# Separate query and key buffers, each reloaded on its own, in a fused attention and gated feed-forward kernel

## The chip, the cores and the metric

The kernel runs on one core of one Trainium2 chip. The metric is the device time of one launch in microseconds (us). Three runs before the change gave 353.80, 353.83 and 354.33 us, median 353.83. The profiled execution spans 352.2 us from its first to its last instruction, with a mean granted TensorE clock of 0.997.

Names used below: TensorE is PE in the profile, its weight loads PEld, VectorE DVE, ScalarE ACT, GpSimd POOL, SyncE SP. A "q" after an engine's name (SPq) is its sequencer, which issues transfers and waits for semaphores.

## The reference, cut to what matters

```python
# q, k, v: (8, 12, 448, 64) f32 ; x: (3584, 768)
q_n, k_n = rmsnorm(q, g_q), rmsnorm(k, g_k)           # over the last 64
attn = softmax(q_n @ k_n.T / 8)                       # 96 heads, 448 x 448
x = (attn @ v).transpose(0, 2, 1, 3).reshape(3584, 768)
a, b = x @ w1, x @ w2                                 # (768, 1024) each
out = (a * b) @ w3 @ w_out                            # (1024, 1024), (1024, 768)
```

Nothing lies between the two last products, so the kernel multiplies the weights w3 and w_out once (w34) and applies the result.

## The kernel before, in words

**Tiles.** The work is cut into 24 "quads" of four heads (three quads make one of the 8 batch entries). A quad's queries and keys are loaded as two transfers of 448 KB into one array `qk_sb`, of which there are three, used in turn (`qk_bufs[i % 3]`, line 308; the second axis of the array tells query from key). So quad i+3 reloads the array of quad i.

**Preparation of a quad** (`plan_prep`, line 455). ACT squares queries, then keys (L464, tile `sq`); DVE sums them (L471, `ssq`); ACT makes the factor by a logarithm and an exponential (L480, L483, `al`); DVE scales queries and keys, in two pieces each (L494, `qks`), and multiplies the queries by the gains (L503). The first five quads (`N_PE_T`) are transposed on TensorE (L1123) and copied out of PSUM into `qkT` (L358 on DVE or L352 on ACT); the others by a DMA transpose that SP issues (L561).

**Attention of a quad.** Seven score passes on TensorE (L679, four matmuls of 64x64 weights and 448 columns each) into two PSUM banks, each followed by an exponential on ACT (L701, into `P` or `Pr`). Then the products with the values and the sums of the rows (L745 and L766), the reciprocals on ACT (L788, L789) and the multiplication into `xT` on DVE (L808), which frees the banks. These products are mostly made for two quads together.

**Feed-forward.** When three quads of a batch entry are in `xT`, its products with w1 and w2 become available, and later those with w34. All of them, and w3 by w_out at the start, run through `do_pass` (L868): four matmuls of 64x64 weights, into a pair of banks. A pair of sums changes its row halves midway, and the change goes through a no-operation on SP or POOL (L852), called a hand-over below. Results leave PSUM by L352 or L358 into `half`, or by L949 (the product a times b, `abT`). Stores are issued by SP (L1005).

**What sets the order.** No engine's order is written out by hand. While the program is built, a planner (`Planner`, line 46) keeps a list of jobs, each with an assumed duration, a rank and conditions; it always takes the job that can start first, and so fixes each engine's order. TensorE takes what `pe_try` (line 1241) offers: scores, a feed-forward pass, a transpose, value products. On the chip each engine runs its list strictly in that order, waiting on semaphores. Where an assumed time is missed on the chip, TensorE stands at the head of its list although later work could run. A few constants steer `pe_try`: `STARVED` (few waiting pairs, below which scores are taken more eagerly) and `HOLD` (if set, value products of two quads wait while a pair of sums is open and no other pair could start).

**Loads.** The weights, the values and the queries and keys of quads 1 to 5 go through POOL, in the order of `POOL_ORDER` (o is a part of w_out, w of w3, a of w1, b of w2, q and v with the quad's number). From quad 6 on SP loads queries and keys. The load of quad i+3 is planned in `complete` (L565), when queries and keys of quad i are both scaled, and may start at `qk_free[i % 3]`, which is set when the last of the four scaling pieces is done. Values are held in four buffers (`v_sb`, L407).

Of the kernel before, what the change touches and what calls it, by code (L numbers as in the profile page):

```python
# [8 lines left out]
FP = mybir.dt.float32  # L9
# [3 lines left out]
AF = mybir.ActivationFunctionType  # L13
# [7 lines left out]
SEM = 0.05  # L21
# [174 lines left out]
def kernel(  # L196
# [15 lines left out]
    B, H, S, D = q.shape  # L212
    NP = 128
# [31 lines left out]
    MARGIN = 0.25  # L245
    LOW = 2
    PV_BANKS = 6
    HOLD = 0
    SOON = 0
    STARVED = 4  # L250
    HUNGRY = 0.6
    ONE = 0
    PARTS = ((2, 4, 6, 8), (2, 4, 6, 8), (4, 8))
# [3 lines left out]
    STOCK = 14  # L257
    PACE = 1.7
    POOL_ORDER = (
        "o0 w0 w1 w2 o1 o2 o3 q1 v0 w3 w4 q2 w5 a0 v1 w6 w7 v2 a1 v3 q3 a2 b0 b1 q4 q5 b2".split()  # L260
    )
    ON_POOL = (1, 2, 3, 4, 5)
    IN_PARTS = (6, 7, 8)
    FIRST = 3.5
    THIN_FROM, THIN = 8, 2.5
    QUIET = 0.5

    w1s = const.tile([128, CM, DFF], BF, name="w1s")
# [23 lines left out]
    def next_of(kind):  # L292
# [13 lines left out]
    warm_t = const.tile([128, 512], BF, name="warm_t")  # L306
    eps_t = const.tile([NP, 1], FP, name="eps_t")
    qk_bufs = [
        const.tile([NP, 2, 2, NJ, D], FP, name="qk_sb" + str(z)) for z in range(3)
    ]  # L310
    v_bufs = [
        const.tile([NP, HQ, J, D], BF, name="v_sb" + str(z)) for z in range(4)
# [7 lines left out]

    bank_at = [0.0] * 8
    landed = [{"q": INF, "k": INF, "v": INF} for _ in range(NQ)]
    qk_free = [0.0] * 3
    v_free = [0.0] * 4
    qkT_at = [[INF, INF] for _ in range(NQ)]
    qkT_used = [INF] * NQ
# [35 lines left out]
    def load_qk(i, which, eng, x0=0, x1=2):  # L362


        b, m = divmod(i, NQB)
        src = (q, k)[which][b, HQ * m : HQ * (m + 1)]
        return eng.dma_start(
            out=qk_bufs[i % 3][:, which, x0:x1].rearrange("p x j d -> p x (j d)"),
            in_=src.rearrange("(x g) (p j) d -> (g p) x (j d)", x=2, j=NJ)[:, x0:x1],
        )  # L370

    def plan_load_qk(i, key=None):
        eng, queue = (nc.gpsimd, "POOL") if i in ON_POOL else (nc.sync, "SP")

        def thin():

            left = sum(x[1] for x in plan.moving["SP"])
            return 0.0 if i < THIN_FROM or left < THIN else INF

        parts = 2 if i in IN_PARTS else 1  # L380
        for which in range(2):
            got = []

            def done(t, which=which, got=got):
                got.append(t)
                landed[i]["qk"[which]] = all_of(got, parts)

            for n in range(parts):
                x0, x1 = 2 * n // parts, 2 * (n + 1) // parts
                add(  # L390
                    queue, {"SP": 0.4, "POOL": 0.75}[queue],
                    (QUAD * i - 30 if key is None else key) + which * 0.01 + n * 0.001,
                    lambda which=which, x0=x0, x1=x1: load_qk(i, which, eng, x0, x1),
                    needs=[lambda: qk_free[i % 3] + (1.0 if i > 5 else 0.0), thin],
                    done=done, moves=(1.35 / parts, 0.086),
                )

# [57 lines left out]
    def plan_prep(i):  # L455
# [5 lines left out]
        def sq(t, x0, x1):  # L461
            if ("sq", t) not in s:
                s["sq", t] = prep_pool.tile([NP, 2, NJ, D], FP, tag="sq", name="sq")
            nc.scalar.activation(  # L464
                out=s["sq", t][:, x0:x1], in_=src[:, t, x0:x1], func=AF.Square
            )

        def red(t, x0, x1):
# [18 lines left out]
        def scale(t, x):  # L487
            if "qkT" not in s:
                s["qkT"] = qkT_pool.tile([128, 2, NJ, NP], BF, tag="qkT", name="qkT")
            if "qks" not in s:  # L490
                s["qks"] = prep_pool.tile(
                    [NP, 2, NJ, 2, D], BF, tag="qks", name="qks"
                )
            nc.vector.tensor_tensor(  # L494
                out=s["qks"][:, t, :, x],
                in0=src[:, t, x],
                in1=s["alpha"][:, t, x].unsqueeze(2).broadcast_to([NP, NJ, D]),
                op=MULT,
            )
# [65 lines left out]
        def complete(t, z):  # L565
            scaled_at[i][t] = z + SEM
            if max(scaled_at[i]) < INF and i + 3 < NQ:
                if i + 3 not in ON_POOL:
                    plan_load_qk(i + 3)
                plan_prep(i + 3)  # L570
            if not pe:
                add(
                    "SP", 1.3, key - 8 + t, lambda: send(t),
                    needs=[lambda: scaled_at[i][t]],
                    done=sent(t), moves=(1.6, 0.026),
                )

        def scaled(t):
            def done(z):
                scaled_x[t].append(z)  # L580
                if len(scaled_x[0]) + len(scaled_x[1]) == 4:
                    qk_free[i % 3] = z + SEM
                if len(scaled_x[t]) == 2:
                    if t == 0 and not pe:
                        add(
                            "DVE", 0.58, key - 11 + 0.5, by_g,
                            needs=[lambda: consts_at["g"]],
                            done=lambda y: complete(0, y),
                        )
                    else:  # L590
                        complete(t, z)

            return done
# [458 lines left out]
    def do_last(t, z):  # L1052
# [17 lines left out]
                    )  # L1070
        took = 2 * CF * pass_us(w) + into("l")
        bank_at[z] = bank_at[z + 1] = INF
        spare = qk_bufs[0].rearrange("p w x j d -> p (w x j d)")
        o_sb = spare[:, x * NH : (x + 1) * NH].rearrange("p (z n) -> p z n", z=1)
        ends = []

# [337 lines left out]
```

## Time and profile before

| part of the span (us) | what runs | PE, DVE, ACT busy (us) | busy share of the 16 DMA engines, GB/s |
|---|---|---|---|
| 0 to 60 | start, w3 by w_out, first quads | 57.70, 37.17, 48.14 | 1.06, 242 |
| 60 to 120 | attention and feed-forward | 59.42, 50.84, 56.28 | 0.92, 184 |
| 120 to 180 | the same | 59.48, 46.22, 53.81 | 0.99, 196 |
| 180 to 222 | the same, last query and key loads | 41.55, 30.50, 38.09 | 0.92, 193 |
| 222 to 288 | last quads | 66.00, 31.63, 51.24 | 0.43, 84 |
| 288 to 345 | feed-forward alone | 57.00, 9.72, 12.91 | 0.19, 51 |

The busy columns are sums over the stretch. A DMA share is the mean of 16 engines; it can pass 1 where packets overlap. Over the whole span PE is busy 344.3 us of 352.2 (98%), ACT 261.9 (74%), DVE 206.8 (59%) and POOL 76.9 (22%). A busy PE is not PE at its peak: matmuls are pipelined, and the time of one matmul contains waiting for those ahead of it.

How the transfers stand in the profile: SP issues the query loads of quads 6 and up (15 of 448 KB, median 5.0 us from issue to landing, and 7 of half the size) and as many key loads (4.9 us); 38 DMA transposes (4.4 us) and 48 stores (3.4 us) stand in the same list. POOL's five query and five key loads, at the start, take 12.3 and 12.4 us.

### The profile page before, as it was taken

To read this page: it belongs to the slowest core of one execution; us is meant where nothing else is said; L and a number is where in the kernel's file an instruction comes from. 1 tells how busy PE (TensorE), PEld (TensorE's weight loads), DVE (VectorE), ACT (ScalarE), POOL (GpSimd) and SP (SyncE) were. 2 spreads that over 40 slices of the span, in tenths; PEclk is the share of its full clock that TensorE was granted. 3 is DMA by queue.
4 is the path that set the end of the run, shared out by engine and by line. 5 is a ranking of instruction groups with operands and counts; after the bars stand their busy time and mean duration, and the time that the engine had idled before them with its cause. 6 is when DMAs were issued, how large, how long until landed. Compare 5 with 4: busy or idle time off the path is not lost.

```text
span 352.2 us, 16197 instructions
## 1 busy us (share of the span) xinstructions
PE 344.3 (98%) x7374; PEld 225.6 (64%) x7374; DVE 206.8 (59%) x293; ACT 261.9 (74%) x375; POOL 76.9 (22%) x134
## 2 busy tenths in 40 slices
PE   8999999999999999999999999999999999999995
PEld 3766656657655756569856575565665656666674
DVE  5379377997989287894969758566643321222100
ACT  4779979989899989897889898777876942222122
POOL 8366720304212223113041031330130000000000
PEclk9999999999999999999999999999999999999998
DMA  8999999599997999988998879852690014100054
GB/s 198 240 273 190 236 306 246 102 184 259 197 202 171 200 160 238 208 161 182 203 247 142 215 102 252 218 72 38 116 176 6 4 47 108 33 2 2 5 165 151
DMA packets 68488, 55.11 MB, mean 156 GB/s; under 512 B 45060, under 2 KB 62372, under 8 KB 68420
## 3 DMA queue, kind: packets, MB, share of 16 engines
q1 hardware_dynamic: 49440, 35.33, 43.4%
q0 software_dynamic: 18048, 16.92, 27.8%
q10 hardware_dynamic: 932, 1.84, 1.5%
q8 instruction: 57, 0.93, 1.1%
q14 instruction: 11, 0.09, 0.1%
HBM read 46.66 MB, written 11.01 MB: 164 GB/s over the span
## 4 chain that ended last, share of the span: by engine, by line
PE 79%; DMA 7%; ACT 5%; DVE 4%; SPq 2%; issue 2%; POOL 2%; DVEq 0%; POOLq 0%; ACTq 0%
PE ps_all L868 59%; PE ps_all L766 9%; PE ps_all L679 8%; DMA w_outs<-in_moe_w_out_dram 3%; ACT P L701 2%; DMA qk_sb<-in_k_dram 2%; PE ps_all L745 2%; DMA qk_sb<-in_q_dram 2%; DVE qks L494 1%; DVE xT L808 1%; PE ps_all L1064 1%; ACT sq L464 1%; ACT half L352 1%; POOL w_outs L448 1%; SPq L561 1%
## 5 line engine op out<-in xcount | busy, mean ns | idle before, releaser
L701 ACT ACTIVATE P<-ps_all 128x896 bf16<-128x896 f32 x114 | 99.4, 922 | 12.0 <-PE ps_all L679 11.6
L407 POOL DMA_DIRECT2D v_sb<-in_v_dram x96 | 57.2, 616 | 177.6 <-PE ps_all L679 90.1
L868 PE MATMUL ps_all<-xT,w2s 64*64 64x448 bf16 x1536 | 89.0, 349 | 0.9 <-DVE xT L808 0.4
L868 PE MATMUL ps_all<-xT,w1s 64*64 64x448 bf16 x1536 | 89.1, 349 | 0.1
L868 PE MATMUL ps_all<-w34s,abT 64*64 64x384 bf16 x1728 | 80.5, 323 | 0.0
L352 ACT ACTIVATE half<-ps_all 128x896 bf16<-128x896 f32 (+1 forms) x38 | 33.3, 877 | 49.4 <-PE ps_all L868 49.3
L949 DVE TENSOR_TENSOR abT<-ps_all,half 128x896 bf16<-128x896 f32 x32 | 34.9, 1089 | 54.8 <-PE ps_all L868 54.6
L868 PEld LDWEIGHTS <-abT 64*64 64x64 bf16 x1728 | 55.1, 107 | 17.3 <-issue 0.7
L868 PEld LDWEIGHTS <-w2s 64*64 64x64 bf16 x1536 | 48.6, 107 | 25.9 <-issue 1.8
L868 PEld LDWEIGHTS <-w1s 64*64 64x64 bf16 x1536 | 47.7, 107 | 25.0 <-POOLq L852 0.9
L679 PE MATMUL ps_all<-qkT 64*64 64x448 bf16 x672 | 62.3, 352 | 0.8 <-ACT Pr L701 0.4
L471 DVE TENSOR_REDUCE ssq<-sq 128x14 f32<-128x896 f32 (+1 forms) x50 | 51.3, 1041 | 18.6 <-ACT sq L464 18.6
L494 DVE TENSOR_TENSOR qks<-qk_sb,al 128x448 bf16<-128x448 f32 x96 | 55.9, 618 | 1.4 <-ACT al L483 1.4
L464 ACT ACTIVATE sq<-qk_sb 128x896 f32<-128x896 f32 (+1 forms) x50 | 45.3, 922 | 2.4 <-DMA qk_sb<-in_k_dram 1.2
L808 DVE TENSOR_TENSOR xT<-ps_all,r 128x448 bf16<-128x448 f32 x48 | 27.7, 618 | 13.2 <-ACT r L789 10.3
L679 PEld LDWEIGHTS <-qkT 64*64 64x64 bf16 x672 | 23.2, 106 | 14.2 <-issue 4.9
L868 PE MATMUL ps_all<-w_outs,w3T 64*64 64x384 bf16 x512 | 25.1, 323 | 0.8 <-DVE w3T L358 0.5
L701 ACT ACTIVATE w_outs<-ps_all 128x896 bf16<-128x896 f32 x24 | 21.6, 912 | 5.2 <-PE ps_all L679 4.8
L766 PE MATMUL ps_all<-P,v_sb 128*32 128x448 bf16 x456 | 25.0, 352 | 0.0
L766 PEld LDWEIGHTS <-v_sb 128*32 128x32 bf16 x592 | 15.8, 97 | 12.2
L701 ACT ACTIVATE Pr<-ps_all 128x896 bf16<-128x896 f32 x24 | 22.1, 921 | 0.1
L358 DVE COPY half<-ps_all 128x768 f32<-128x768 f32 x13 | 12.4, 955 | 13.9 <-PE ps_all L868 13.2
(65 smaller groups left out, 212.8 us busy)
## 6 DMA issues: line engine op xcount, KB each, us to landing
out_dram<-half SPq DMA_DIRECT2D x48, 192.0 KB, 3.4
qk_sb<-in_q_dram SPq DMA_DIRECT2D x15, 448.0 KB, 5.0
qk_sb<-in_k_dram SPq DMA_DIRECT2D x15, 448.0 KB, 4.9
v_sb<-in_v_dram POOLq DMA_DIRECT2D x48, 64.0 KB, 3.8
v_sb<-in_v_dram POOLq DMA_DIRECT2D x48, 48.0 KB, 4.1
qk_sb<-in_q_dram POOLq DMA_DIRECT2D x5, 448.0 KB, 12.3
qk_sb<-in_k_dram POOLq DMA_DIRECT2D x5, 448.0 KB, 12.4
w3s<-in_moe_w_dram POOLq DMA_DIRECT2D x8, 256.0 KB, 6.9
```

What stands on the lines that cost most here:

```text
L352: nc.scalar.activation(out=out, in_=in_, func=AF.Copy, scale=1.0 if by is None else by)
L358: nc.vector.tensor_copy(out=out, in_=in_)
L407: nc.gpsimd.dma_start(out=v_bufs[i % 4][p0 : p0 + HP, g::2, 0 : j1 - j0].rearrange("p h j d -> p h (j d)"), in_=src[:, g::2, j0:j1].rearra ...
L464: nc.scalar.activation(out=s["sq", t][:, x0:x1], in_=src[:, t, x0:x1], func=AF.Square)
L471: nc.vector.tensor_reduce(out=s["ssq"][:, t, x0:x1], in_=s["sq", t][:, x0:x1], axis=AX, op=ADD)
L494: nc.vector.tensor_tensor(out=s["qks"][:, t, :, x], in0=src[:, t, x], in1=s["alpha"][:, t, x].unsqueeze(2).broadcast_to([NP, NJ, D]), op=MULT,
L679: nc.tensor.matmul(out=sc[HP * c : HP * c + HP, u, 0:S].rearrange("p (j s) -> p j s", j=NJ), lhsT=qkT[u * D : (u + 1) * D, 1, j, cols], rh ...
L701: lambda: nc.scalar.activation(out=dst, in_=sc[:, :, 0:S], func=AF.Exp),
L766: nc.tensor.matmul(out=ps_all[hd * HALF : (hd + 1) * HALF, z, 0:S], lhsT=value_weights(i, hd, j, kind), rhs=s["P"][:, hd, j, :] if j < NF ...
L808: lambda: nc.vector.tensor_tensor(out=xT[b][:, 2 * m + kind - 1, :], in0=ps, in1=s["r"], op=MULT),
L868: mm = nc.tensor.matmul(out=ps_all[64 * h : 64 * h + 64, p.bank + z, 0 : p.n], lhsT=lhsT[64 * r : 64 * r + 64, 64 * h : 64 * h + 64], rhs= ...
L949: nc.vector.tensor_tensor(out=abT[bp][:, f0 : f0 + 2, odd * S : (odd + 1) * S], in0=ps_all[:, z : z + 2, 0:S], in1=a_sb[b, f0], op=MULT,)
```

## The change

The array of queries and keys becomes two arrays, one for each. A load then depends only on the instructions that read its own half: the queries of quad i+3 are planned as soon as both pieces of the queries of quad i are scaled, the keys likewise. This is meant to let loads start earlier, without more memory. The change also gives `POOL_ORDER` a new order, sets `HOLD` from 0 to 1 and `STARVED` from 4 to 6. Since the planner decides from all of these, every engine's order changes with them.

```diff
-    HOLD = 0
+    HOLD = 1
-    STARVED = 4
+    STARVED = 6
     POOL_ORDER = (
-        "o0 w0 w1 w2 o1 o2 o3 q1 v0 w3 w4 q2 w5 a0 v1 w6 w7 v2 a1 v3 q3 a2 b0 b1 q4 q5 b2".split()
+        "w0 o0 o1 w1 w2 o2 q1 o3 v0 w3 v1 w4 w5 q2 v2 w6 a0 w7 q3 a1 v3 a2 b0 b1 q4 q5 b2".split()
     )
...
     qk_bufs = [
-        const.tile([NP, 2, 2, NJ, D], FP, name="qk_sb" + str(z)) for z in range(3)
+        [const.tile([NP, 2, NJ, D], FP, name="qk"[w] + "_sb" + str(z)) for w in range(2)]
+        for z in range(3)
     ]
...
-    qk_free = [0.0] * 3
+    qk_free = [[0.0] * 2 for _ in range(3)]
...
-    def plan_load_qk(i, key=None):
+    def plan_load_qk(i, key=None, parts_of=(0, 1)):
...
-        for which in range(2):
+        for which in parts_of:
...
-                    needs=[lambda: qk_free[i % 3] + (1.0 if i > 5 else 0.0), thin],
+                    needs=[
+                        lambda which=which: qk_free[i % 3][which] + (1.0 if i > 5 else 0.0), thin
+                    ],
...
         def complete(t, z):
             scaled_at[i][t] = z + SEM
             if max(scaled_at[i]) < INF and i + 3 < NQ:
-                if i + 3 not in ON_POOL:
-                    plan_load_qk(i + 3)
                 plan_prep(i + 3)
...
                 scaled_x[t].append(z)
-                if len(scaled_x[0]) + len(scaled_x[1]) == 4:
-                    qk_free[i % 3] = z + SEM
                 if len(scaled_x[t]) == 2:
+                    qk_free[i % 3][t] = z + SEM
+                    if i + 3 < NQ and i + 3 not in ON_POOL:
+                        plan_load_qk(i + 3, parts_of=(t,))
```

The remaining edits follow the new shape of `qk_bufs` in the code that reads it.

More of the change, by code (lines that the diff above doesn't have):

```diff
@@ L264 @@
     FIRST = 3.5
-    THIN_FROM, THIN = 8, 2.5
+    THIN_FROM = 8
+    THIN = 2.5
     QUIET = 0.5
@@ L367, in load_qk @@
         return eng.dma_start(
-            out=qk_bufs[i % 3][:, which, x0:x1].rearrange("p x j d -> p x (j d)"),
+            out=qk_bufs[i % 3][which][:, x0:x1].rearrange("p x j d -> p x (j d)"),
             in_=src.rearrange("(x g) (p j) d -> (g p) x (j d)", x=2, j=NJ)[:, x0:x1],
         )
-    def plan_load_qk(i, key=None):
+    def plan_load_qk(i, key=None, parts_of=(0, 1)):
         eng, queue = (nc.gpsimd, "POOL") if i in ON_POOL else (nc.sync, "SP")
@@ L464, in sq @@
             nc.scalar.activation(
-                out=s["sq", t][:, x0:x1], in_=src[:, t, x0:x1], func=AF.Square
+                out=s["sq", t][:, x0:x1], in_=src[t][:, x0:x1], func=AF.Square
             )
@@ L495, in scale @@
                 out=s["qks"][:, t, :, x],
-                in0=src[:, t, x],
+                in0=src[t][:, x],
                 in1=s["alpha"][:, t, x].unsqueeze(2).broadcast_to([NP, NJ, D]),
@@ L1072, in do_last @@
         bank_at[z] = bank_at[z + 1] = INF
-        spare = qk_bufs[0].rearrange("p w x j d -> p (w x j d)")
+        spare = qk_bufs[0][0].rearrange("p x j d -> p (x j d)")
         o_sb = spare[:, x * NH : (x + 1) * NH].rearrange("p (z n) -> p z n", z=1)
```

## The prediction

> **What bounds the kernel now.** I read the busy table first, then the groups by line, then the waits, the chain and the timeline.
>
> ```profile
> PE 344.3 (98%) x7374; PEld 225.6 (64%) x7374; DVE 206.8 (59%) x293; ACT 261.9 (74%) x375; POOL 76.9 (22%) x134
> ...
> PE 79%; DMA 7%; ACT 5%; DVE 4%; SPq 2%; issue 2%; POOL 2%; DVEq 0%; POOLq 0%; ACTq 0%
> ```
>
> The first line is each engine's busy time, the second the shares in the chain that ended last. TensorE fills both. As 98% busy says nothing of its rate, I count passes. In the timeline a pass of four matmuls of 448 columns is followed by the next after 0.19 us (12 matmuls at 109.91, the next group at 110.48: three passes, 0.57), a pass of 384 columns after 0.163 (8 of them in 1.30 us between 28.68 and 29.98). The groups hold 1536 + 1536 feed-forward matmuls of 448 columns (768 passes, 145 us), 1728 + 512 of 384 (560 passes, 91 us), 672 for scores (168 passes, 32 us), 888 in the value products (222 passes, 42 us). The rest sums (264 in eights, 6 us), transposes (7) and the last tile (3) follow. That is 326 us of work at the full rate. To it come 8.6 us before the first transpose, 4.1 after the last matmul's end (348.1 to 352.2), and some 5.1 for 49 changes between kinds of work (0.105 us each: value products at 24.33, transpose at 24.62, of which 0.187 is the pass). What is left, about 8 us, is dummy matmuls, small change, and **stalls**. Going through the starts of the matmuls I find 5.9 us of stalls over 0.04 us; the larger ones stand at 13.1, 17.5, 21.0 (0.3 each), 25.9 (0.58), 51.0 (0.48), 103.7 (0.29), 115.9 (0.62 and 0.23), 145.8 (0.29), 151.3 (0.22), 152.2 (0.72), 185.8 (0.53) and 191.8 (0.29). From 222 us on there is 0.14 in all. **So no reordering can gain more than about 6 us, and all of it lies in the first 195 us.**
>
> Two stretches of the chain of waits concern the edited loads:
>
> ```profile
> 139.66 1.75 SPq L367
> ...
> 141.54 7.17 DMA qk_sb<-in_k_dram
> ...
> 148.79 0.96 ACT sq L464
> ...
> 152.46 0.55 DVE xT L808
> ...
> 153.05 2.05 PE ps_all L868 x37
> ```
>
> ```profile
> 177.46 1.82 SPq L561
> ...
> 179.32 5.38 DMA qk_sb<-in_q_dram
> ...
> 184.75 0.83 issue
> 185.58 0.74 ACT Pr L701
> ```
>
> Columns are start, duration, what. In the first a key load is issued at 141.54 and needs 7.17 us (median 4.9); the square, the sum and the scaling run late, push the multiplications into `xT` back on DVE, and those hold PSUM banks. In the second a query load lands at 184.70, ACT waits for it at the head of its list, and the exponential behind it comes late. TensorE pays here:
>
> ```profile
> 152.15 0.53 PE L868 MATMUL ps_all<-xT,w2s 64*64 64x448 bf16 x2
> ...
> 153.05 1.29 PE L868 MATMUL ps_all<-xT,w2s 64*64 64x448 bf16 x21 [0.37 <-DVE xT L808]
> ```
>
> ```profile
> 186.53 1.33 PE L868 MATMUL ps_all<-xT,w2s 64*64 64x448 bf16 x24 [0.35 <-ACT Pr L701]
> ```
>
> From 152.15 to 153.05 are 0.90 us for one pass of 0.19: 0.72 lost. The group before the second line began at 185.63 with two passes (0.38), so 0.52 is lost. With 0.22 at 151.34 (a score followed after 0.41) the loads explain about **1.5 us** of the 5.9.
>
> **What the Trainium skill says.** "Perfetto Trace Analysis", section "Identifying the Most-Contended Engine", says that matmul busy time is a poor measure of the distance to the peak; the trace agrees (98% busy, 326 of 352 us of work). "DMA: Bandwidth & Descriptors", "Issuing engines are not separate DMA queues": transfers of all issuers share the 16 engines and interleave. It agrees: POOL's 448 KB loads, issued amid weights, take 12.3 us, SP's 5.0. The same page, "Queues, rings and completion order", has an engine going round its queues packet by packet; hence a load issued earlier takes bandwidth from transposes and stores under way. "VectorE: DVE Perf Modes", "The perf-mode tier table", gives a copy and a multiplication by one scalar the same rate; it is the price for one operation below.
>
> **The change part by part**, with the built order of instructions of both programs at hand.
>
> *Matmuls.* The counts of all real passes are equal; 22 dummies of 256 columns become 16. Each is 0.107 us (13 end after 1.53): **-0.64**. They go because w0 now comes first on POOL: its transpose runs ahead of the queries', and four w3-by-w_out passes stand before the first score. Queries of quad 0 are not on POOL, so the first transpose stays near 8.6.
>
> *Changes of kind.* 57 instead of 49, as w3 transposes are strewn among passes: 8 x 0.105 = **+0.84**.
>
> *Hand-overs.* A half that follows its own first half at once stalls 0.29 (21.0, 103.7, 145.8); three such places become two: **-0.29**.
>
> *PSUM copies.* Five query copies of the first quads move from ACT (1.009 us each) to DVE, one key copy moves the other way, and one copy into `half` moves to ACT. ACT loses 5.0 - 1.0 - 0.9 = 3.1 us. DVE's scaled copy from PSUM is not in the trace: low end the plain copy of that shape, 0.617, high end the unscaled rounding copy of f32, 1.087. I take 0.62, since the page prices both alike; DVE gets 5 x 0.62 - 0.62 - 1.09 = +1.4 us (up to +3.7). DVE has 37 of 60 us in that stretch, so neither end shows by itself; behind these copies stand sums and scalings, and through them the next transposes. I book zero.
>
> *POOL order.* What precedes q1 shrinks by o3 (384 KB), what precedes q3 by v3 and a1 (some 0.7 MB); q2 gets w5 and v1 ahead of it (0.48 MB). At 242 GB/s these are about 1.6 and 3 us earlier, 2 us later. In 0 to 60 us filler passes are plentiful, so I book zero, and up to +1 in a rival.
>
> *Query and key loads.* SP still issues the same transfers, with no more bytes. The query load may start when two pieces are scaled rather than four: two scalings of 0.618 and often an `xT` multiplication of 0.62 between them, 1.2 to 2 us earlier, in places ahead of a transpose in SP's list that it followed before. Behind an early load in that list stand the transposes and stores, 0.4 to 0.5 us of issue each time. The transposes have room: only 0.4 us in the whole trace were waited for them. The two late loads above were late by 1.2 us (ACT's wait for keys) and 0.4 (for queries), less than the lead gained. So the **-1.5** goes.
>
> *HOLD and STARVED* add no instruction. They choose between scores and passes; ACT, which they feed, is 90% busy until 180 us but has 57 us of feed-forward after it. Zero.
>
> *The rest of the stalls*, 5.9 - 1.5 - 0.9 (the three hand-overs) = 3.5 us, come from mismatches between assumed and real times. The first half has a new order, so they fall elsewhere; I assume the same sum. The last 723 passes, which begin at 215 us in the trace, stand in the same order in both programs, so from there to the end should take as long.
>
> Sum: -0.64 + 0.84 - 0.29 - 1.5 = -1.6; 353.83 - 1.6 = 352.2.
>
> **The rivals.**
> - *The gain is eaten* (0.20). Engines are 0.92 to 0.99 busy from 60 to 222 us, so early queries only slow the keys and the transposes, and landing times stay. For: 7.17 us for a load in a crowded stretch. Against: the mean there is 190 GB/s, below the 242 of the start. Then -0.1: 353.7.
> - *A new wait* (0.24), on the slower side. The new order has two runs of four scores in a row where before three was the longest; a fourth score waits for banks that ACT frees at 0.92 us apiece. At 115.9 a run of three cost 0.85, so two of four cost about 1 more; q2's 2 us or DVE's added copies can cost another 1. With the loads unhelped, 353.7 + 2 = 355.7; with half of it 354.7.
> - *Most stalls go* (0.12). Scores at work early, fewer collisions: 80% of the 5.9 us, -4.7 + 0.2 (dummies and changes): 349.3.
> - *My forecast* (0.44): 352.2, with +-1 for the stalls that move.
>
> **How the numbers follow.** Faster by over 0.2% (below 353.1): most of my case (0.40), the last rival (0.12), a little of the first (0.06): 0.58. Slower (above 354.5): 0.21 of the new wait, 0.04 of the others: 0.25. Within: 0.17. The range goes from near the last rival, 349.6, to most of the new wait, 355.3.
>
> **What would show it.** The chain should no longer hold query or key loads of 5 to 7 us with ACT behind them, and ACT's waits for them (2.3 us together) should shrink. Stalls over 0.04 us should sum to about 4. Dummies should end by the first score, at about 11.4 or a little earlier; the last 137 us should keep their length. I am wrong if loads land no earlier against the squares that need them, if the early quads' transposes wait for `qks`, or if scores wait for ACT in the runs of four.

## The result, and the profile after

The changed kernel takes **356.54 us** (median of six runs, 354.96 to 357.55); the kernel before takes 353.87 on the same chip (six runs, 353.58 to 355.33). The ratio is 1.0066, with a 95% interval of 1.0038 to 1.0093: slower by 2.3 us by the ratio (2.7 by the medians), where 1.6 us less was forecast. The time lies above the predicted range. Both profiled executions, 352.2 us of span before and 355.2 after, are ordinary runs of their kernels; a span is about 1.8 us shorter than the time of the same run. The figures below come from these spans.

The page after, its busy table and its chain of waits by engine:

```profile
span 355.2 us, 16178 instructions
...
PE 345.9 (97%) x7368; PEld 224.8 (63%) x7368; DVE 208.5 (59%) x296; ACT 259.4 (73%) x372; POOL 76.7 (22%) x134
...
PE 82%; DMA 7%; ACT 5%; POOL 3%; SPq 1%; DVE 1%; issue 0%; POOLq 0%
```

Little here shows where the time went: TensorE has six instructions fewer, though it is busy 1.6 us longer, ACT has 2.5 us less work, and the DMA share of the chain is the same. So I took the matmul starts apart by the method of the prediction. All passes of real work but the last tile take 319.1 us in both kernels, counted at 0.187 us for a pass of 448 columns and 0.160 for one of 384 (the prediction's 326 takes slightly longer steps, and the last tile in). What differs:

| part of the span, us | before | after | difference |
|---|---|---|---|
| up to the first transpose, and dummies after it | 8.62 + 0.96 | 7.64 + 1.71 | -0.2 |
| changes between kinds of work (49 and 57), and other gaps too small to be stalls | 8.60 | 9.44 | +0.84 |
| stalls over 0.04 us | 5.83 (21 of them) | 8.11 (26) | +2.28 |

These sum to +2.9, the difference of the spans being 3.0. Of the stalls, 1.31 us are added in the first 45 us, 1.07 in the next 45 and 0.39 in the third; from 135 to 225 us there are 0.5 fewer, and after that as many as before. The next table has the time at which TensorE has done so much work, that is, at which its passes add up to so many us at these prices:

```
work done, us       5     20     40     60    100    140    200    300    end
before           15.3   32.1   54.0   74.7  117.3  160.2  223.1  325.6  352.2
after            16.8   33.9   56.4   77.9  120.6  163.1  226.1  328.6  355.2
behind by         1.5    1.8    2.4    3.2    3.3    2.9    3.0    3.0    3.0
```

**In these two executions all of the loss is there by 78 us.** From 200 us of work to the end both need 129.1 us. One execution of each does not fix the early loss closely: in other profiles below in which TensorE starts with the same passes, 40 us of work are done at 53.9 to 55.0 us (six with the start of before) and at 55.1 to 56.9 (four with the changed start).

The larger of the new stalls are of three kinds. The first is a query or key load that comes late. From the chain of waits of the kernel after (start, duration, what):

```profile
7.87 12.89 DMA w_outs<-in_moe_w_out_dram
...
24.04 8.04 DMA k_sb<-in_k_dram
32.09 0.95 ACT sq L468
33.04 0.81 ACT P L704
...
175.01 4.79 DMA k_sb<-in_k_dram
179.82 0.95 ACT sq L468
```

and TensorE's timeline beside it:

```profile
30.55 2.61 PE L871 MATMUL ps_all<-w_outs,w3T 64*64 64x384 bf16 x60
33.90 0.38 PE L682 MATMUL ps_all<-qkT 64*64 64x448 bf16 x4 [0.74 <-ACT P L704]
```

`q2` stands behind `w5` and `v1` in the new `POOL_ORDER`. The key load of quad 2 is issued at 24.04 where it was at 20.91, and lands at 32.08. ACT waits for it at the head of its list, then squares, and the exponential behind the square starts only at 33.04; the score that wants its bank stands at 33.90. The 15 passes before it end at 33.0 (15 x 0.163), so 0.9 us is lost. The second stretch (175.01) is the kind of wait that the change was meant to remove: a key load issued late by SP, with ACT's square right behind it.

The second kind is a run of scores. From the timeline after:

```profile
52.54 1.17 PE L682 MATMUL ps_all<-qkT 64*64 64x448 bf16 x12
53.95 0.38 PE L682 MATMUL ps_all<-qkT 64*64 64x448 bf16 x4 [0.23 <-ACT P L704]
...
118.68 0.57 PE L682 MATMUL ps_all<-qkT 64*64 64x448 bf16 x8
119.49 0.38 PE L682 MATMUL ps_all<-qkT 64*64 64x448 bf16 x4 [0.24 <-ACT P L704]
120.30 0.38 PE L682 MATMUL ps_all<-qkT 64*64 64x448 bf16 x4 [0.42 <-ACT Pr L704]
```

Three passes are 0.56 us of work, and the fourth stands 1.41 after the first: 0.85 lost. In the other run of four 0.44 and 0.62 are lost. Together that is 1.9 us, where before the prediction put 0.85 on a run of three at 115.9 (0.62 between its scores, 0.23 at the pass behind it).

The third is the start. Stalls of 0.27 to 0.56 stand at 13.1, 14.2 and 15.5 us, where scores and w3 transposes alternate at the pace of ACT's exponentials; w3-by-w_out passes stood between these scores before. A hand-over at 12.4 costs 0.28, and the last part of `w_out` 0.16 at 20.5. That part (`o3`, behind `q1` in the new order) lands at 20.76; before it did so at 17.88, and TensorE waited 0.27 for it at 17.5. So the wait for `o3` has not grown; what a later `o3` can change is which passes the planner has at hand. The load in the chain of the kernel before:

```profile
6.14 11.74 DMA w_outs<-in_moe_w_out_dram
```

ACT's waits for query and key loads, from the table of waits (us in total, times, longest), first of the kernel before, then after:

```profile
ACT sq L464 <- DMA qk_sb<-in_k_dram: 1.2, 1, 1.2
ACT sq L464 <- DMA qk_sb<-in_q_dram: 1.1, 3, 0.5
```

```profile
ACT sq L468 <- DMA q_sb<-in_q_dram: 3.0, 3, 1.6
ACT sq L468 <- DMA k_sb<-in_k_dram: 3.0, 3, 1.3
```

They grew from 2.3 to 6.0 us. The freed loads are not needed for that: with the new `POOL_ORDER` alone, in the second experiment below, they are 7.2, with the two constants alone 4.7. In the table of DMA issues the key loads' median from issue to landing is 5.9 us, before 4.9; that of the queries 5.1, before 5.0.

### The profile page after: what moved, and what is told of

Its sections match the earlier page's. It is cut to its first block, busy times and chain, and to the rows that moved or that the text cites. A ratio compares the mean times of both kernels' runs of the same rounds, so it can differ in the third digit from the quotient of the medians.

```text
span 355.2 us, 16178 instructions
## 1 busy us (share of the span) xinstructions
PE 345.9 (97%) x7368; PEld 224.8 (63%) x7368; DVE 208.5 (59%) x296; ACT 259.4 (73%) x372; POOL 76.7 (22%) x134
## 3 DMA queue, kind: packets, MB, share of 16 engines
q1 hardware_dynamic: 49440, 35.33, 43.2%
## 4 chain that ended last, share of the span: by engine, by line
PE 82%; DMA 7%; ACT 5%; POOL 3%; SPq 1%; DVE 1%; issue 0%; POOLq 0%
PE ps_all L871 59%; PE ps_all L769 11%; PE ps_all L682 8%; DMA w_outs<-in_moe_w_out_dram 4%; DMA k_sb<-in_k_dram 4%; ACT P L704 3%; PE ps_all L748 2%; SPq L565 1%; POOL w3s L446 1%; PE ps_all L1067 1%; ACT sq L468 1%; POOL w_outs L452 1%; SPq L1008 1%; PE ps_all L1126 1%; ACT Pr L704 0%
## 5 line engine op out<-in xcount | busy, mean ns | idle before, releaser
L704 ACT ACTIVATE P<-ps_all 128x896 bf16<-128x896 f32 x114 | 98.3, 922 | 12.3 <-PE ps_all L682 12.0
L871 PE MATMUL ps_all<-xT,w1s 64*64 64x448 bf16 x1536 | 88.1, 349 | 0.2
L871 PEld LDWEIGHTS <-abT 64*64 64x64 bf16 x1728 | 52.5, 107 | 19.6 <-issue 0.6
L871 PEld LDWEIGHTS <-w1s 64*64 64x64 bf16 x1536 | 49.5, 107 | 24.0 <-issue 0.7
L871 PEld LDWEIGHTS <-w2s 64*64 64x64 bf16 x1536 | 47.5, 107 | 24.9 <-SPq L855 0.6
L682 PEld LDWEIGHTS <-qkT 64*64 64x64 bf16 x672 | 24.2, 106 | 17.4 <-issue 9.3
L498 DVE TENSOR_TENSOR qks<-q_sb,al 128x448 bf16<-128x448 f32 x48 | 28.0, 617 | 2.3 <-ACT al L487 2.3
L498 DVE TENSOR_TENSOR qks<-k_sb,al 128x448 bf16<-128x448 f32 x48 | 27.8, 617 | 1.2 <-ACT al L487 1.2
L468 ACT ACTIVATE sq<-q_sb 128x896 f32<-128x896 f32 (+1 forms) x25 | 22.8, 914 | 3.1 <-DMA q_sb<-in_q_dram 3.0
L468 ACT ACTIVATE sq<-k_sb 128x896 f32<-128x896 f32 (+1 forms) x25 | 22.8, 914 | 3.0 <-DMA k_sb<-in_k_dram 3.0
```

What stands on the lines that cost most here:

```text
L468: nc.scalar.activation(out=s["sq", t][:, x0:x1], in_=src[t][:, x0:x1], func=AF.Square)
L498: nc.vector.tensor_tensor(out=s["qks"][:, t, :, x], in0=src[t][:, x], in1=s["alpha"][:, t, x].unsqueeze(2).broadcast_to([NP, NJ, D]), op=MULT,
L682: nc.tensor.matmul(out=sc[HP * c : HP * c + HP, u, 0:S].rearrange("p (j s) -> p j s", j=NJ), lhsT=qkT[u * D : (u + 1) * D, 1, j, cols], rh ...
L704: lambda: nc.scalar.activation(out=dst, in_=sc[:, :, 0:S], func=AF.Exp),
L871: mm = nc.tensor.matmul(out=ps_all[64 * h : 64 * h + 64, p.bank + z, 0 : p.n], lhsT=lhsT[64 * r : 64 * r + 64, 64 * h : 64 * h + 64], rhs= ...
```

## The experiments

The questions in order: which part of the edit is slower; whether the loads matter at all; whether anything but the planned order acts; and whether the early loss has a cause that can be mended. `before` in each line is the kernel before, timed beside it. Ratios carry their 95% intervals.

### The edit in its parts

The change falls into separate arrays with own loads ("split"), the POOL order, and the two constants. The first experiment is the split alone, the changed kernel with the three old settings:

```diff
-    HOLD = 1
+    HOLD = 0
-    STARVED = 6
+    STARVED = 4
-        "w0 o0 o1 w1 w2 o2 q1 o3 v0 w3 v1 w4 w5 q2 v2 w6 a0 w7 q3 a1 v3 a2 b0 b1 q4 q5 b2".split()
+        "o0 w0 w1 w2 o1 o2 o3 q1 v0 w3 w4 q2 w5 a0 v1 w6 w7 v2 a1 v3 q3 a2 b0 b1 q4 q5 b2".split()
```

> Separate query and key arrays with loads of their own; POOL order, HOLD and STARVED as before. Theory O (the new POOL order costs the time): within 0.5 us of the kernel before, or faster, and the first 45 us as in it. Theory S (earlier loads of queries crowd the others, so ACT waits longer for keys): slower by 2 us or more, with ACT's waits for queries and keys well above the 2.3 us of before. Theory P (any new plan has other mismatches with the chip): anywhere from -1 to +3 us, with the lost time in other places than in the changed kernel.

Measured: 359.31 us, before 354.22; 1.0133 (1.0099 to 1.0167).

The second is the kernel before with the new POOL order only:

```diff
-        "o0 w0 w1 w2 o1 o2 o3 q1 v0 w3 w4 q2 w5 a0 v1 w6 w7 v2 a1 v3 q3 a2 b0 b1 q4 q5 b2".split()
+        "w0 o0 o1 w1 w2 o2 q1 o3 v0 w3 v1 w4 w5 q2 v2 w6 a0 w7 q3 a1 v3 a2 b0 b1 q4 q5 b2".split()
```

> The kernel before with the new POOL order alone. Theory O: slower by about 2.5 us, nearly all of it in the first 55 us, where TensorE starts the same passes as in the changed kernel and should show the same stalls (12 to 17 us: 1.7; near 33: 0.9; near 53: 0.8). Theory S: within 0.5 us of the kernel before. Theory P: the first 45 us as in the changed kernel, and after them -1 to +2 us of stalls in new places.

Measured: 357.21; 1.0080 (1.0053 to 1.0107).

The third is both of these, the changed kernel with `HOLD = 0` and `STARVED = 4`:

> The changed kernel with HOLD back at 0 and STARVED back at 4. The changed kernel took 356.5. If the two constants do nothing: 356.5 within 0.7. If they lengthen it: 355 or less. Theories O and S both say slower than before by 2 us or more; theory P leaves -1 to +3.

Measured: 356.02; 1.0053 (1.0031 to 1.0075). Against the whole change, 1.0066, the intervals overlap, so the two constants change nothing in it that can be told here.

The fourth is the kernel before with the two constants only:

```diff
-    HOLD = 0
+    HOLD = 1
-    STARVED = 4
+    STARVED = 6
```

> The kernel before with HOLD 1 and STARVED 6 alone. Theories O and S: within 0.5 us of the kernel before. Theory P: the first 302 passes stand as before, and the rest, newly planned, loses another sum, so 1 us or more away in either direction.

Measured: 358.68; 1.0113 (1.0080 to 1.0147).

**Each part by itself is slower than all together, and they do not add:** +1.33% and +0.80% make +0.53%, and with the constants, +1.13% by themselves, +0.66%. So no part "costs" a fixed amount. What they share is that each gives the planner another decision, after which it writes other lists. Of the theories, O (the POOL order costs the time) fails with the first run, which is slower with the old order, and S (crowding by earlier loads) with the second and the fourth, which are slower without loads that start earlier. P (any new plan has other mismatches) is left, but its range of -1 to +3 us was too small for the 4.7 of the first.

### Do the loads matter?

Two kernels keep every list of their parent and cut the bytes of the query and key loads from quad 3 on to a seventh (the other six are not loaded). The edit in the kernel before (the changed kernel has the same in its own arrays):

```diff
+        n = D if i >= 3 else NJ * D
-            out=qk_bufs[i % 3][:, which, x0:x1].rearrange("p x j d -> p x (j d)"),
+            out=qk_bufs[i % 3][:, which, x0:x1].rearrange("p x j d -> p x (j d)")[:, :, 0:n],
-            in_=src.rearrange("(x g) (p j) d -> (g p) x (j d)", x=2, j=NJ)[:, x0:x1],
+            in_=src.rearrange("(x g) (p j) d -> (g p) x (j d)", x=2, j=NJ)[:, x0:x1, 0:n],
```

> The kernel before, its order on every engine unchanged, but the query and key loads of quads 3 to 23 move one seventh of their bytes (the first of the seven rows of each partition; the rest keeps old data, so the output is not the reference's). Late loads can then hold nobody. Theory L (the difference between the two kernels is ACT waiting for loads): about -1.5 us, the two places that the prediction traced to loads, at 151 to 153 and 186. Theory M (the lists differ in other mismatches between assumed and real times): also -1 to -1.5, since the kernel before has only 2.3 us of such waits on ACT.

> The changed kernel with the same cut of its query and key loads, its order unchanged. Theory L: the stalls that the waits caused go, -3 us or more against the changed kernel (356.5), so it ends within 0.8 us of the kernel before with cut loads. Theory M: -1 us or less, and it stays 2 us or more behind the kernel before with cut loads: the stalls at 12 to 16, 47 to 53 and 118 to 120 us remain.

Measured: the kernel before with cut loads 352.52, the changed one 355.01, before itself 353.99; ratios 0.9959 (0.9944 to 0.9973) and 1.0018 (1.0003 to 1.0033). ACT's waits for these loads, of the first and then of the second:

```profile
ACT sq L465 <- DMA qk_sb<-in_q_dram: 0.6, 1, 0.6
```

```profile
ACT sq L469 <- DMA q_sb<-in_q_dram: 0.6, 1, 0.6
ACT sq L469 <- DMA k_sb<-in_k_dram: 0.3, 1, 0.3
```

The waits shrink from 2.3 to 0.6 and from 6.0 to 0.9 us. In the kernel before, the stalls between 135 and 225 us fall from 2.42 to 0.69: those that the prediction traced to two late loads are gone. The kernel before gains 1.5 us (0.41%), the changed one about 1.7 (from 1.0066 to 1.0018), and **the gap between them stays at 2.5 us**. The loads were worth what the prediction put on them. From quad 3 on they are just not what separates the two kernels (theory L asked for 3 us and an equal time), and the change did not relieve them. The loads of quads 1 and 2 are whole here, so the late `q2` is still in.

### Does anything act but the order?

In this experiment the kernel before gets the two arrays, with the planner as it was. The built program has all instructions in the same order, and each waits for the same semaphores.

```diff
-        const.tile([NP, 2, 2, NJ, D], FP, name="qk_sb" + str(z)) for z in range(3)
+        [const.tile([NP, 2, NJ, D], FP, name="qk"[w] + "_sb" + str(z)) for w in range(2)]
+        for z in range(3)
...
-            out=qk_bufs[i % 3][:, which, x0:x1].rearrange("p x j d -> p x (j d)"),
+            out=qk_bufs[i % 3][which][:, x0:x1].rearrange("p x j d -> p x (j d)"),
```

> The kernel before with queries and keys in arrays of their own and nothing else: the planner still plans the loads together, so every engine's list is that of before. If the separate arrays themselves do something on the chip (other waits, other places in SBUF): 0.7 us or more away from the kernel before. If the change acts through the plan alone (theory P): within 0.5 us.

Measured: 354.02, before 353.80; 1.0002 (0.9976 to 1.0027). **The arrays by themselves do nothing.** A load waited already before for those instructions alone that touch the bytes it overwrites; the one array had held back only the planner, whose `qk_free` knew one time for both halves. So, as far as these runs show, the change acts through the lists alone: their order and, with it, which engine makes a copy.

The controls disturb the plan without any purpose. `TO_ENGINE` is the time that the planner assumes from one engine to the next; the first of these is the kernel before, the second the changed one, the third again the kernel before with a smaller step.

```diff
-TO_ENGINE = 0.23
+TO_ENGINE = 0.235
```

> The kernel before, with one assumed time of the planner (TO_ENGINE) moved from 0.23 to 0.235 us: no load, buffer or operation differs, and the first 262 passes stand as before; the plan after them is another. If the plan of before is an ordinary one: within 1 us on either side. If it is an uncommonly lucky one (theory P): slower by 1 to 4 us, as for the three partial changes.

> The changed kernel with the same nudge: the first 471 passes stand as in it. If the new plan is an ordinary one: within 1.5 us of 356.5 on either side. If the change itself costs the time, no nudge helps: 356 or more.

```diff
-TO_ENGINE = 0.23
+TO_ENGINE = 0.231
```

> The kernel before with TO_ENGINE at 0.231 instead of 0.23: 8 small exchanges among the passes 828 to 980, TensorE's first 828 and last 844 passes as before. If what a new plan costs grows with how much of the list is new: within 0.7 us of the kernel before. If any departure costs the whole amount: 2 us slower.

Measured: 356.90, 1.0089 (1.0056 to 1.0121), where the first 262 passes stay as they were and the rest is planned anew; 355.60, 1.0053 (1.0034 to 1.0072), for the changed kernel; 354.54, 1.0005 (0.9987 to 1.0022) for the small step, which exchanges neighbours in eight places among passes 828 to 980. A change of 5 ns in an assumed time costs the kernel before as much as the whole edit; one of 1 ns, which alters little of the list, costs nothing that can be told. In the first of them, stalls between 90 and 135 us went from 1.24 to 2.86 and those between 225 and 270 from 0.14 to 1.60: no load order was edited, and the stalls just fall elsewhere.

### Is the early loss o3's?

The order `q1` before `o3` is the most visible thing in the first 20 us, so four kernels move it. First, the changed kernel with the old beginning of the order, `o3` still behind `q1`; its first 95 passes stand as in the kernel before, its last 1757 as in the changed one:

```diff
-        "w0 o0 o1 w1 w2 o2 q1 o3 v0 w3 v1 w4 w5 q2 v2 w6 a0 w7 q3 a1 v3 a2 b0 b1 q4 q5 b2".split()
+        "o0 w0 w1 w2 o1 o2 q1 o3 v0 w3 v1 w4 w5 q2 v2 w6 a0 w7 q3 a1 v3 a2 b0 b1 q4 q5 b2".split()
```

> The changed kernel with the first eight weight parts of the POOL order back as before (o0 w0 w1 w2 o1 o2, then q1 o3 as changed). TensorE's first 95 passes then stand as in the kernel before, and its last 1757 as in the changed kernel, so the two differ in the first 16 us or so alone. If the stalls there (1.5 us, scores that wait for ACT with few w3-by-w_out passes between them) are a part of what was lost: 1.0 to 1.8 us faster than the changed kernel (356.4), so 354.6 to 355.4. If they only move what would be waited for later: within 0.4 us of the changed kernel.

Measured: 356.85, before 354.41; 1.0089 (1.0052 to 1.0126): no gain. Five us of work are done at 15.3 us, as in the kernel before; then the timeline has

```profile
17.20 2.31 PE L871 MATMUL ps_all<-w_outs,w3T 64*64 64x384 bf16 x52
20.12 1.82 PE L871 MATMUL ps_all<-w_outs,w3T 64*64 64x384 bf16 x40 [0.61 <-DMA w_outs<-in_moe_w_out_dram]
```

13 passes end at 19.3 (13 x 0.163), and 0.8 us passes until `o3` is there. The better start reaches the same wall earlier. At 200 us of work the kernel is only 0.4 us ahead of the changed one.

Next, the kernel before with the new beginning, but `o3` ahead of `q1`:

```diff
-        "o0 w0 w1 w2 o1 o2 o3 q1 v0 w3 w4 q2 w5 a0 v1 w6 w7 v2 a1 v3 q3 a2 b0 b1 q4 q5 b2".split()
+        "w0 o0 o1 w1 w2 o2 o3 q1 v0 w3 w4 q2 w5 a0 v1 w6 w7 v2 a1 v3 q3 a2 b0 b1 q4 q5 b2".split()
```

> The kernel before, loads planned together, with the first weight parts in the new order (w0 o0 o1 w1 w2 o2, then o3 q1 as before). The first 89 passes stand as in the changed kernel. If the new start costs time by itself: 1 to 1.8 us behind the kernel before at the same work done at 20 us; the rest is newly planned, so the whole is 1 to 4 us slower.

Measured: 357.03; 1.0084 (1.0052 to 1.0117). Its profile does 40 us of work by 54.4 us, 0.4 behind the kernel before where the changed kernel is 2.4 behind. That supported `o3`. The whole is as slow all the same: from there on it loses elsewhere.

The first of these two again, with the cut loads of above, asks whether late loads ate what its start gained:

> The changed kernel with the old start of the POOL order (its first 95 passes as before, its last 1757 as changed) and with query and key loads of quads 3 to 23 cut to a seventh of their bytes (the rest keeps old data, so the output is not the reference's). The changed kernel with cut loads ran at 1.0018 of the kernel before; the old start alone gained nothing (1.0089). If the 1.2 us that the old start saves up to 140 us were given back in waits for loads near 175 to 183 us: they stay here, so 0.8 to 1.4 us faster than the changed kernel with cut loads, a ratio of 0.998 to 0.9995. If the start gives nothing in the end: 1.0018 within 0.0012.

Measured: 354.54, before 354.25; 1.0001 (0.9983 to 1.0018). It lies below the changed kernel with cut loads (1.0018, 1.0003 to 1.0033), but the intervals overlap. That the loads took the gain back is likely, and not shown.

Then the exchange within the changed kernel, `o3` alone:

```diff
-        "w0 o0 o1 w1 w2 o2 q1 o3 v0 w3 v1 w4 w5 q2 v2 w6 a0 w7 q3 a1 v3 a2 b0 b1 q4 q5 b2".split()
+        "w0 o0 o1 w1 w2 o2 o3 q1 v0 w3 v1 w4 w5 q2 v2 w6 a0 w7 q3 a1 v3 a2 b0 b1 q4 q5 b2".split()
```

> The changed kernel with one exchange in POOL_ORDER: o3 back ahead of q1. The first 89 TensorE passes stand as in the changed kernel, the rest is planned anew. Theory A, early loss by o3: the last part of w_out lands near 18 us instead of 20.8, the w3-by-w_out passes can fill the waits of the first scores, and TensorE has done 40 us of work 1 to 2 us earlier than in the changed kernel (56.4 us there, 54.0 in the kernel before). If nothing is given back, the time is then 354 to 355.5. Theory B, every order planned anew costs some stalls wherever they fall: the early part is better but the rest of the gap moves to later stretches, and the time stays at 355.5 to 358. Rival C, the start has nothing to do with o3: 40 us of work are done at 56 us or later.

Measured: 363.52, before 353.71; **1.0255** (1.0224 to 1.0286), the slowest of all and outside every expectation. The timeline at the start, first of TensorE, then of POOL, whose next issues wait for the landings of `o2` and `o3`:

```profile
16.29 0.39 PE L682 MATMUL ps_all<-qkT 64*64 64x448 bf16 x4
17.86 1.46 PE L871 MATMUL ps_all<-w_outs,w3T 64*64 64x384 bf16 x29 [1.19 <-DMA w_outs<-in_moe_w_out_dram]
...
18.11 0.57 POOL L446 DMA_DIRECT2D w3s<-in_moe_w_dram  x1 [2.79 <-DMA w_outs<-in_moe_w_out_dram]
19.69 0.59 POOL L411 DMA_DIRECT2D v_sb<-in_v_dram  x1 [1.01 <-DMA w_outs<-in_moe_w_out_dram]
```

`o3` lands at 19.16, 1.6 us earlier than in the changed kernel. But the part ahead of it, `o2`, lands at 17.82, 1.4 us later than there (16.46), and it is `o2` for which TensorE stands still for 1.4 us. In the kernel above with the new beginning and `o3` ahead of `q1`, where the first loads are the same, `o2` came at 16.25 and this wait is not there; why it came late here is open. 40 us of work are done only at 60.4 us, against 56.4. From 81 to 89 us two DMA transposes cost 1.8 and 1.4 us more; the second takes 8 us (median of the changed kernel: 4.6), from the chain:

```profile
80.56 0.52 DVE xT L811
81.08 8.01 DMA qkT<-qks
...
89.13 0.57 PE ps_all L682 x8
```

Last, the other suspect of the first 40 us, quad 2's keys: `q2` ahead of `w5` and `v1`.

```diff
-        "w0 o0 o1 w1 w2 o2 q1 o3 v0 w3 v1 w4 w5 q2 v2 w6 a0 w7 q3 a1 v3 a2 b0 b1 q4 q5 b2".split()
+        "w0 o0 o1 w1 w2 o2 q1 o3 v0 w3 w4 q2 w5 v1 v2 w6 a0 w7 q3 a1 v3 a2 b0 b1 q4 q5 b2".split()
```

> The changed kernel with q2 put back ahead of w5 and v1 in POOL_ORDER, o3 still behind q1. The first 113 TensorE passes stand as in the changed kernel. Theory A, quad 2's keys: they land 2 to 3 us earlier than 32.1, ACT's wait for them and the 0.9 us stall of TensorE at 32.8 go, and the loss between 20 and 40 us of work (0.6 us against the kernel before) shrinks to 0 to 0.3; by itself that gives 355 to 356. Theory B, every order planned anew: other stalls appear, 355.5 to 358. Rival C, the load is late for another reason (bandwidth): it lands at 31.5 or later and the stall stays.

Measured: 358.18; 1.0123 (1.0101 to 1.0145). ACT squares these keys at 27.4 instead of 32.1, and the stall of 0.9 at 32.8 is gone. In its place stand 0.62 at 31.7, where a transpose waits for a bank that ACT frees, and 0.49 at 32.6, where a part of w3 has not come. The chain has the part, the timeline the wait:

```profile
28.43 5.02 DMA w3s<-in_moe_w_dram
```

```profile
33.49 0.62 PE L1148 MATMUL ps_all<-ident,w3s 128*128 128x128 bf16 x8 [0.32 <-DMA w3s<-in_moe_w_dram]
```

40 us of work are done at 56.6 us, as late as in the changed kernel (56.4). The keys were what TensorE waited for; when they came earlier, it waited for a bank and a weight in their place.

### Can a new plan beat the kernel before?

Three more kernels set several constants and the POOL order together, the first and the third on the changed kernel, the second on the kernel before. Their edits, cut to the core:

```diff
-TO_ENGINE = 0.23
+TO_ENGINE = 0.22
-    QUAD = 13.0
+    QUAD = 13.5
-        "w0 o0 o1 w1 w2 o2 q1 o3 v0 w3 v1 w4 w5 q2 v2 w6 a0 w7 q3 a1 v3 a2 b0 b1 q4 q5 b2".split()
+        "w0 w1 o0 o1 o2 w2 o3 q1 v0 w4 w3 w6 q2 w5 a0 v1 a1 v2 v3 w7 q3 b0 b1 a2 q4 b2 q5".split()
...
```

> The changed kernel, early loads kept, with another POOL order and other constants of the planner (TO_ENGINE, QUAD, LOW, STARVED, HUNGRY, AHEAD_W3, STOCK, PACE, FIRST, QUIET), taken from some thousands of plans because TensorE's list ends earliest by the planner's own reckoning. Theory P (the change costs only because its plan has more idle time in it): 354 or less, at or below the kernel before, with stalls over 0.04 us on TensorE of 6 us or less. If early loads do harm whatever the plan: 355.5 or more.

```diff
-TO_ENGINE = 0.23
+TO_ENGINE = 0.231
-    QUAD = 13.0
+    QUAD = 13.1
-        "o0 w0 w1 w2 o1 o2 o3 q1 v0 w3 w4 q2 w5 a0 v1 w6 w7 v2 a1 v3 q3 a2 b0 b1 q4 q5 b2".split()
+        "w1 w0 o0 w2 o1 o2 o3 q1 v0 w3 w4 q2 w5 v1 w6 a0 v3 a1 v2 w7 q3 a2 b0 q4 b1 q5 b2".split()
...
```

> The kernel before, loads planned together, with constants and a POOL order taken in the same way. Theory P: 354 or less, like the early loads replanned, since neither kind of load is better. If early loads help once both have a good plan: 0.7 us or more behind that kernel.

```diff
-TO_ENGINE = 0.23
+TO_ENGINE = 0.235
-    QUAD = 13.0
+    QUAD = 12.5
-        "w0 o0 o1 w1 w2 o2 q1 o3 v0 w3 v1 w4 w5 q2 v2 w6 a0 w7 q3 a1 v3 a2 b0 b1 q4 q5 b2".split()
+        "w1 w0 w2 o1 o0 o2 o3 q1 v0 w4 q2 w5 v1 w3 a0 w6 w7 v3 q3 v2 a1 a2 b0 q4 b1 b2 q5".split()
...
```

> Early loads with a third set of constants and POOL order, from the same search, started elsewhere. Theory P: within 1 us of the other replanned kernel, so about 353.5 to 355. If how near the chip comes to the plan is mere luck: anywhere from 353 to 358.

Measured beside 353.80: 356.35, 1.0078 (1.0047 to 1.0109); 355.52, 1.0049 (1.0031 to 1.0067); 358.82, 1.0155 (1.0113 to 1.0197). None beats the kernel before, though the planner reckons their ends earliest, so its own reckoning does not rank lists this finely. Part of the loss can be the clock: the third's profile has a granted clock of 0.71 between 30 and 40 us (the first's 0.83), after ten us of which TensorE was busy for 6.3 (7.7). At 0.71 these ten us cost 2.9. Yet the third took 358.64 in a run with a mean clock of 0.999 too, so the clock does not set its median.

With full loads, 15 lists planned otherwise than before have run, the changed kernel among them. 14 are slower, by 0.5 to 2.6%; the one with eight exchanges of neighbours is the same. These are not 15 independent draws: several share long stretches with the old list or with the changed one.

## Why the prediction was wrong

Point by point, by its own steps.

- **The loads, -1.5 us: failed.** The amount was right: with cut loads the kernel before gains 1.5 us, and the two stalls named are the ones that vanish. The step that failed is "1.2 to 2 us earlier". It was reckoned for a query load and then set against both late loads, of which the key load carried 0.94 of the 1.5 us. In the trace every quad's keys are scaled after its queries, so the keys' half comes free when the last of the four pieces is done, just as before: the edit gives key loads no lead of their own. By the issue times in the trace, the last twelve query and twelve key loads start 2.4 us later on average than before, while TensorE is 3.0 us behind: by work done they are 0.6 us earlier, queries and keys alike, with single ones 3 us later or over 6 us earlier. That a load may start earlier was taken for its starting earlier, and that for its landing before the square that needs it. ACT's waits rose from 2.3 to 6.0 us. The prediction also has an early load taking turns, between queues, with transposes and stores under way. In the profile of the kernel before SP's loads, transposes and stores share one queue, q1: it moves 35.33 MB, and they are 35.1 by their sizes. Nothing was booked on this.
- **The rest of the stalls, "the same sum": failed, and this is as large a miss as the loads.** Of the 8.11 us of stalls after, the cut loads are worth about 1.7 and the hand-overs 0.99, so some 5.4 are left (an estimate) where 3.5 were booked. The kernel before is not a typical draw: of 15 other plans none has been measured faster. A fair forecast for the stalls is the level of newly planned lists, not that of the list in hand. The penalty is shown only as a spread; why this one list fits the chip so well is not shown. How the old list was arrived at is not on record; one that was kept because it ran well would look the same.
- **POOL order, booked zero as "filler passes are plentiful": failed.** Over 60 us they are plentiful, but all of the early ones are w3-by-w_out passes, which need their parts of `w_out` and w3, and the new list has few of them between the first scores. Of the 2.8 us of stalls before 45 us in the profile after (1.5 before), 2.4 end at an exponential, 0.9 of these behind the late `q2`; 0.28 end at a hand-over and 0.16 at `o3`.
- **`HOLD` and `STARVED`, zero:** within the changed kernel right (1.0053 without them, 1.0066 with). By themselves on the kernel before they cost 1.13%: a replanned list again, not an operation.
- **Changes of kind, +0.84: right**, 9.44 against 8.60.
- **Dummies, -0.64: mis-sized.** (13 in 1.53 us are 0.118 each, not 0.107; the price is right all the same, 9 of them fill 0.96.) 16 instead of 22 run, but the queries' first transpose starts at 8.97 instead of 8.62, and the net of start and dummies is -0.23.
- **Hand-overs, -0.29: not delivered.** The two places forecast are there (0.28 at 12.4, 0.29 at 149.8), but a third stall, 0.42 at 146.9 behind a score, ends at a hand-over too: 0.99 in all, before 0.88.
- **PSUM copies, zero: nearly right.** The scaled copy takes 0.68 us on DVE where the plain copy of that shape, taken for it, takes 0.62; the Trainium skill's "VectorE: DVE Perf Modes", "The perf-mode tier table", gives both the same rate, so the measurement, 10% more, decides. DVE is busy 1.7 us longer (+1.4 forecast), ACT 2.5 us less (-3.1 forecast). No stall found ends at one of these copies.
- **The last 723 passes keep their length: right**, 129.1 us from 200 us of work on in both.

The rival "a new wait" is nearest. Two of its terms are in the trace: the runs of four scores cost 1.9 us against 0.85 of a run of three before, and `q2`'s late load costs 0.9. Its sum, 355.7, is 0.8 below the time. What the runs add is that these waits could not be taken away singly: with `q2` brought forward the wait changed its name and the time did not fall. I gave it 0.24, and the forecast of my own 0.44, on the strength of a saving whose amount was right and whose delivery was not looked at.

**What is settled:** the arrays alone do nothing; the bytes of the loads from quad 3 on do not make the difference; what acts is the planned lists, and 14 of the 15 others tried cost 0.5% or more. **What stays open:** which property of the old list makes it fit, and whether a search over plans by measurement on the chip would find a better one. Of the changed kernel's loss the trace says where it lies, not that mending one place would win it back; the attempts, at `o3`, at the start and at `q2`, did not.

## What to carry to other kernels

Where lists are planned ahead of time and the bound engine is 97% busy, judge an edit to the planner by running a control beside it: the same kernel with an assumed time moved by a few ns. Here 5 ns cost 0.9%, so a gain from freer loads would have to be worth more than this before it could show, and a list that has measured well is worth keeping when data structures change (the separate arrays with the old lists run at 1.0002). Before a load's earlier start is booked as a gain, ask which loads the edit frees at all, and look in the new lists at how far each one's consumer moved too.

## What the runs showed of the hardware beyond expectation

- Two arrays instead of one changed no wait in the built program and no time (1.0002, 0.9976 to 1.0027): the halves of one array had been independent already.
- The same transfers land after very different times. `o3`, 384 KB issued by POOL, took 11.7 us before and 12.9 after; the five key loads that POOL issues took 5.4 to 15.4 us before and 7.0 to 12.6 after. A DMA transpose took 8.0 us in one crowded stretch, where the median is 4.4 and the longest of the kernel before 7.1. And with the same loads ahead of it `o2` landed at 16.25 us in one kernel and at 17.82 in another. Against these spreads stand stalls of 0.2 to 0.9 us.
- The start varies between executions with the same beginning: 5 us of work are done at 15.3 us in the profile of the kernel before, and at 16.1 with the cut loads, where the list and the loads of the first three quads are the same.
